# Two spare PSUM banks as working space for weight conversion and a product, in the last two blocks of a middle stage

## The chip, the cores and the metric

The kernel runs on one core of a Trainium2 chip. The metric is the device time of one execution in microseconds (us). Before the change the median of 3 runs is 1579.26 us (1579.03 to 1581.0).

## What is computed

Pooled attention feeds two groups of dense layers. In short:

```
k_p, v_p = mean of k, v over groups of 8 positions        # 576 -> 72 positions
attn     = softmax(q k_p^T / 8) v_p                       # 8 batches, 8 heads, 64 wide
x  = attn as 4608 tokens x 512
a  = x @ w1;  b = x @ w2                                  # 512 -> 1024
x2 = ((a * b) @ w3) @ w_out                               # 1024 -> 1024 -> 512
h  = x2 @ w_in2;  g = h * sigmoid(1.702 h)                # 512 -> 2048
out = g @ w_out2                                          # 2048 -> 512
```

The weights arrive in 64-bit floating point and are turned into 32-bit on the chip. Every 32-bit operand of a product is split in two parts, a rounded high part and the remainder, and each product is three matmuls (high by high, high by low, low by high).

## The kernel before

The program has three stages. The first converts and transposes the weights of the middle layers and runs the first attention groups. The middle stage (lines 547 to 588) goes over 9 blocks of 512 tokens; in each block it goes over 8 slices f of 128 features. For a slice TensorE makes `a` in PSUM bank `wk[0]` and `b` in bank `wk[1]`, 12 matmuls each (lines 566 to 568). ScalarE copies `a` to SBUF (line 573), VectorE multiplies it with `b` out of the bank (line 574), ScalarE writes the high part of the product to `u` and GpSimd the remainder (`split`, lines 95 to 97, called at line 576). Two slices later `x2_step` multiplies `u` with the folded weights into the four `acc` banks, 12 matmuls more. So a slice has 36 matmuls. Attention for later blocks runs between (`tick`) and uses banks `wk[2]` and `wk[3]`; it has ended when the last two blocks begin.

In the last two blocks the middle stage also converts the weights of the third stage: 16 tiles of `w_in2` in the first of the two and 16 of `w_out2` mostly in the second, two tiles a slice (`Conv.step`, lines 146 to 172). For one tile ScalarE scales the upper 32-bit words into a tile `w` in SBUF (line 154) and turns the lower words into integers (line 155); VectorE shifts `w` in place (line 156) and puts the sign bits in (line 159); GpSimd adds the low words (line 162). The tile then goes on a step later: `win_first` and `win_second` (lines 426 to 448) make sums and differences of quarter tiles (line 444), split them (lines 419 and 420) and store them to DRAM; `wout_done` (lines 450 to 456) splits and stores. The subtractions at 420 and 444 and half of those of `wout_done` are VectorE's, the others GpSimd's; both of their operands lie in SBUF.

The third stage (from line 599) takes the memory of the middle one. Its first matmuls need four tiles `g`, loaded at line 737, whose loads wait for the last stores of the middle stage (line 545).

Every engine works through its own instructions in a fixed order and waits on semaphores; DMA transfers are issued by SyncE, in order too. The order on each engine is made by a scheduler when the kernel is built, from the program and its own estimates of durations, so an edit in one line can reorder instructions around it on all engines.

Of the kernel before, what the change touches and what calls it, by code (L numbers as in the profile page):

```python
# [7 lines left out]
F32 = mybir.dt.float32  # L8
F32R = mybir.dt.float32r
U32 = mybir.dt.uint32  # L10
I32 = mybir.dt.int32
AF = mybir.ActivationFunctionType
ALU = mybir.AluOpType
# [9 lines left out]
def pooled_attention_moe_moe2(  # L23
# [18 lines left out]
    nc = tc.nc  # L42
# [11 lines left out]
    NB = NT // T  # L54
# [19 lines left out]
    wk = [ps_p.tile([P, T], F32, name=f"wk{i}", tag=f"bank{i + 4}") for i in range(4)]  # L74
# [7 lines left out]
    def take(shape=(P, 2, T), dtype=F32R):  # L82
        pool, i = free.pop(0)
        t = pool.tile(list(shape), dtype, name=f"s{i}", tag=f"s{i}")
        held[id(t)] = (t, pool, i)
        return t

    def give(*ts):
        for t in ts:
            free.append(held.pop(id(t))[1:])  # L90

    def f32(ap):
        return ap.bitcast(F32)

    def split(dst, src, lo_eng):
        nc.scalar.copy(dst[:, 0], src)  # L96
        lo_eng.tensor_tensor(out=dst[:, 1], in0=src, in1=f32(dst[:, 0]), op=ALU.subtract)  # L97
# [6 lines left out]
    def mm3(o, a, a_sl, b, b_sl, first, last):  # L104

        nc.tensor.matmul(o, a[:, 0, a_sl], b[:, 0, b_sl], start=first, stop=False)  # L106
        nc.tensor.matmul(o, a[:, 0, a_sl], b[:, 1, b_sl], start=False, stop=False)  # L107
        nc.tensor.matmul(o, a[:, 1, a_sl], b[:, 0, b_sl], start=False, stop=last)  # L108

    def col_tile(w, f):  # L110
        return w[:, 2 * f * P:2 * (f + 1) * P].rearrange("(c p) m -> p c m", p=P)

    def row_tile(w, f):
        return w[f * P:(f + 1) * P, :]

    def sl(i, n=P):
        return slice(i * n, (i + 1) * n)

    class Conv:
# [3 lines left out]
        def __init__(self):  # L123
            self.todo, self.staged, self.line = [], [], [None, None]
            self.depth, self.keep = 9, 3

        def add(self, src, turn, done):
            self.todo.append((src, turn, done))
# [17 lines left out]
        def step(self):  # L146

            new = None
            if self.staged:
                t, turn, done = self.staged.pop(0)  # L150
                lo_w, hi_w = t[:, :, 0], t[:, :, 1]
                w = cv_p[0].tile([P, T], F32, name="cv", tag="cv", bufs=4)
                wu = w.bitcast(U32)
                nc.scalar.activation(w, hi_w.bitcast(F32), AF.Copy, scale=2.0 ** -112)
                nc.scalar.activation(lo_w.bitcast(I32), lo_w, AF.Copy, scale=2.0 ** -29)
                nc.vector.tensor_scalar(  # L156
                    out=wu, in0=wu, scalar1=4, scalar2=1,
                    op0=ALU.logical_shift_left, op1=ALU.logical_shift_right)
                nc.vector.scalar_tensor_tensor(  # L159
                    out=wu, in0=hi_w, scalar=0x80000000, in1=wu,  # L160
                    op0=ALU.bitwise_and, op1=ALU.bitwise_or)
                nc.gpsimd.tensor_tensor(  # L162
                    out=w.bitcast(I32), in0=w.bitcast(I32), in1=lo_w.bitcast(I32), op=ALU.add)
                give(t)
                new = [w, turn, done]
            mid, old = self.line
            if mid and mid[1]:
                mid[0] = mid[1](mid[0])
            key = old[2](old[0]) if old else None
            self.line = [new, mid]  # L170
            self.load()
            return key
# [4 lines left out]
    conv = Conv()  # L177
    cv_p = [None]

    with pa_ctx:  # L180
# [7 lines left out]
            out=mask[:, 0], in_=mask[:, 0], compare_op=ALU.is_gt, fill=0.0,  # L188
            base=SK, pattern=[[0, D]], channel_multiplier=-1)
        nc.gpsimd.affine_select(  # L190
            out=mask[:, 1], in_=mask[:, 1], compare_op=ALU.is_ge, fill=0.0,
# [12 lines left out]
            out=ident, in_=ident, compare_op=ALU.is_equal, fill=0.0,  # L204
# [172 lines left out]
        def x_slot(j, c):  # L377
            if (j, c) not in xs:
                xs[j, c] = take()
            return xs[j, c]  # L380
# [3 lines left out]
        def tick():  # L384
            t = tick_n[0]
            tick_n[0] += 1
            n, s = divmod(t, 4)
            if s == 0:
                if 0 <= n - 1 < NG:
                    g4(n - 1)  # L390
                if n == 0:
                    g0(0)
            elif s == 1:
                if n < NG:
                    g1(n)
            elif s == 2:
                if 0 <= n - 1 < NG:
                    g6(n - 1)
                if n < NG:
                    g2(n)  # L400
                    g_va(n)
                if n + 1 < NG:
                    g0(n + 1)
            elif n < NG:
                g3(n)
                g_vb(n)
# [19 lines left out]
        def win_first(f):  # L426
            def done(w):
                hold[0] = w
                units(f, A11, A12, w, nc.vector)
            return done  # L430

        def win_second(f):
            def done(w):
                h = hold[0]
                a11, a12 = h[:, :HU], h[:, HU:]
                a21, a22 = w[:, :HU], w[:, HU:]
                units(f, A21, A22, w, nc.gpsimd)
                c = take((P, 2, T), F32)
                cs = c.rearrange("p a (b m) -> p (a b) m", b=2)
                for o, p0_, p1_, op, eng in (  # L440
                        (0, a21, a22, ALU.add, nc.vector), (2, a11, a21, ALU.subtract, nc.gpsimd),
                        (1, cs[:, 0], a11, ALU.subtract, nc.vector),
                        (3, a12, cs[:, 1], ALU.subtract, nc.gpsimd)):
                    eng.tensor_tensor(out=cs[:, o], in0=p0_, in1=p1_, op=op)
                units(f, S1, S2, c[:, 0], nc.vector)
                units(f, S3, S4, c[:, 1], nc.gpsimd)
                give(c)
            return done

        def wout_done(f):  # L450
            def done(w):
                t = take()
                split(t, w, nc.gpsimd if f % 2 else nc.vector)
                nc.sync.dma_start(wout_d[f], f32(t))
                give(t)
            return done
# [90 lines left out]
        for blk in range(NB):  # L547
            x = [x_slot(blk, c) for c in range(KM)]
            if blk == NB - 2:

                pa_ctx.close()
                pa = pa_ctx.enter_context(tc.tile_pool(name="pc", bufs=1, reuse_waits="tile"))
                cv_p[0] = pa
                free[:0] = [(pa, NSLOT + i) for i in range(NX)]
                for f in range(NP1):
                    conv.add(col_tile(w_in2, f), None, win_first(f))
                    conv.add(col_tile(w_in2, f + NP1), None, win_second(f))
                for f in range(NF2):
                    conv.add(row_tile(w_out2, f), None, wout_done(f))
                conv.depth, conv.keep = 5, 5  # L560
                conv.load()
            for f in range(NF1):
                if conv.busy():
                    conv.step()
                pa_, pb_ = wk[0], wk[1]
                for ps, w in ((pa_, w1_s[f]), (pb_, w2_s[f])):
                    for c in range(KM):
                        mm3(ps, w, sl(c), x[c], slice(0, T), c == 0, c == KM - 1)
                if blk == NB - 1:
                    give(w1_s.pop(f))  # L570
                    give(w2_s.pop(f))
                a = pa.tile([P, T], F32, name="a", tag="a", bufs=2)
                nc.scalar.copy(a, pa_)
                nc.vector.tensor_tensor(out=a, in0=pb_, in1=a, op=ALU.mult)  # L574
                u = u_s[blk, f] = take()
                split(u, a, nc.gpsimd)
                pend.append((blk, f))
                tick()
                if len(pend) > 2:
                    x2_step()  # L580
                tick()
                if conv.busy():
                    conv.step()
            give(*(xs.pop((blk, c)) for c in range(KM)))
# [14 lines left out]
    with tc.tile_pool(name="pb", bufs=1, reuse_waits="tile") as pb, \  # L599
# [146 lines left out]
        for f in range(NF2):  # L746
            bk = bank()
            w = ready.pop(("h", 0, f, 0))
# [23 lines left out]
        for pr in range(1, NPAIR + 1):  # L772
# [3 lines left out]
            for f in range(NP1):  # L776
# [10 lines left out]
                for name, u, b, first in ORDER:  # L787
                    o = B[b][1]
                    s, h = HS[u]
                    w = ready["h", pr, f, s]  # L790
# [90 lines left out]
```

## Time and profile before

| | |
|---|---|
| median of 3 runs | 1579.26 us |
| the profiled execution | 1577.45 us, of which its span is 1575.7 us |
| TensorE (PE) busy | 1500.1 us, 95% of the span |
| VectorE (DVE) busy | 1007.7 us, 64% |
| ScalarE (ACT), GpSimd (POOL) busy | 619.2 us, 617.0 us, 39% each |
| mean granted TensorE clock | 0.976 |

The span is the time from the first to the last instruction; what lies around it is 1.75 us here. TensorE is busy nearly throughout, so time is to be had only where it stands still or its granted clock is low. Times in the rows below are counted from the start of the span. The first of the last two blocks begins near 655 us and the middle stage ends near 816 us. The matmuls of a line overlap, so the distance of their starts, not their duration, is what one costs.

### The profile page before, as it was taken

The page shows a single profiled execution, that of the slowest core. Times are in us where ns is not written, and L with a number is a line of the kernel's source. Part 1 is how long each engine was busy: PE and PEld are TensorE (multiplying, and loading weights), DVE is VectorE, ACT ScalarE, POOL GpSimd, SP SyncE. Part 2 cuts the span into 40 slices and gives each one's busy share as a digit, 9 for nine tenths or more (in the row PEclk, how much of TensorE's full clock was granted, in tenths as well). Part 3 has the DMA queues.
Part 4 walks back from the last instruction along what each step waited for, and adds up shares of the span by engine and source line. Part 5 has one row for each costly group of instructions (what it writes and reads, how often), then busy time and mean ns, then how long its engine had stood idle before and what let it go on. Part 6 is the DMA issues. An engine that isn't in the chain of part 4 may idle for free.

```text
span 1575.7 us, 19586 instructions
## 1 busy us (share of the span) xinstructions
PE 1500.1 (95%) x6728; PEld 1233.7 (78%) x6728; DVE 1007.7 (64%) x1796; ACT 619.2 (39%) x1202; POOL 617.0 (39%) x674
## 2 busy tenths in 40 slices
PE   5976999999999999998979999999999999999998
PEld 3654888888888888876757888888888888888887
DVE  8999987878787877579754234462447244724441
ACT  6775443433333434355534222342225222522331
POOL 7789755444555554479752211100111011101110
PEclk9877999999999999999989999999999999999999
DMA  9972232323232310369769343432434234414310
GB/s 271 242 172 58 55 73 46 72 52 79 49 72 48 78 31 27 121 237 337 305 231 374 100 129 125 133 108 101 127 112 143 92 107 136 147 57 137 117 58 27
DMA packets 225444, 196.33 MB, mean 125 GB/s; under 512 B 158784, under 2 KB 175168, under 8 KB 225344
## 3 DMA queue, kind: packets, MB, share of 16 engines
q1 hardware_dynamic: 224768, 194.03, 41.3%
q8 instruction: 53, 0.87, 0.2%
q10 hardware_dynamic: 576, 1.05, 0.2%
q14 instruction: 47, 0.39, 0.1%
HBM read 150.99 MB, written 44.04 MB: 124 GB/s over the span
## 4 chain that ended last, share of the span: by engine, by line
PE 81%; DVE 8%; DMA 4%; issue 3%; POOL 1%; SPq 1%; ACT 1%; DVEq 0%; POOLq 0%; ACTq 0%
PE bk L644 22%; PE bk L108 8%; PE bk L107 8%; PE bk L106 8%; PE wk L108 7%; PE wk L106 7%; PE wk L107 7%; PE acc L108 3%; PE acc L107 3%; PE acc L106 3%; DVE cv L156 2%; PE wk L258 2%; DVE cv L159 2%; DMA s<-in_moe_w_dram 1%; DVE s L97 1%
## 5 line engine op out<-in xcount | busy, mean ns | idle before, releaser
L644 PE MATMUL bk<-xM,st 128*128 128x512 f32 x1344 | 319.1, 389 | 0.0
L644 PEld LDWEIGHTS bk<-xM,st 128*128 128x128 f32 x1344 | 252.3, 188 | 52.7 <-ACT o L661 0.4
L785 POOL TENSOR_TENSOR g<-g,sg 128x512 f32<-128x512 f32 x64 | 83.4, 1303 | 529.3 <-ACT sg L784 529.3
L106 PE MATMUL wk<-s,s 128*128 128x512 f32 x576 | 228.9, 399 | 15.0 <-DVE a L574 8.3
L107 PE MATMUL wk<-s,s 128*128 128x512 f32 x576 | 226.8, 394 | 2.0 <-DVE s L370 2.0
L108 PE MATMUL wk<-s,s 128*128 128x512 f32 x576 | 226.4, 394 | 1.4 <-DVE s L97 1.4
L107 PE MATMUL bk<-wo,mv 128*128 128x512 f32 x576 | 224.1, 389 | 0.0
L106 PE MATMUL bk<-wo,mv 128*128 128x512 f32 x576 | 223.9, 389 | 0.0
L108 PE MATMUL bk<-wo,mv 128*128 128x512 f32 x576 | 208.8, 389 | 0.0
L293 DVE STREAM_TRANSPOSE p<-s_t 32x160 f32<-32x160 f32 (+1 forms) x560 | 178.4, 319 | 10.8
L97 POOL TENSOR_TENSOR s<-a,s 128x512 fp32r<-128x512 f32 x72 | 96.6, 1341 | 185.6 <-ACT s L96 136.4
L106 PE MATMUL acc<-s,s 128*128 128x512 f32 x352 | 141.4, 407 | 7.1 <-ACT s L96 7.1
L108 PE MATMUL acc<-s,s 128*128 128x512 f32 x352 | 141.8, 403 | 5.1 <-DVE s L97 5.1
L107 PE MATMUL acc<-s,s 128*128 128x512 f32 x352 | 141.0, 400 | 0.9 <-POOL s L97 0.7
L106 PEld LDWEIGHTS wk<-s,s 128*128 128x128 f32 x576 | 108.8, 189 | 40.8 <-DVE a L574 10.6
L108 PEld LDWEIGHTS wk<-s,s 128*128 128x128 f32 x576 | 109.4, 190 | 24.8 <-DVE s L97 1.8
L107 PEld LDWEIGHTS wk<-s,s 128*128 128x128 f32 x576 | 109.5, 190 | 24.3 <-DVE s L370 2.4
L784 ACT ACTIVATE sg<-g 128x512 f32<-128x512 f32 x64 | 40.5, 633 | 217.0 <-DVE g L802 198.0
L107 PEld LDWEIGHTS bk<-wo,mv 128*128 128x128 f32 x576 | 108.1, 188 | 22.5
L106 PEld LDWEIGHTS bk<-wo,mv 128*128 128x128 f32 x576 | 108.1, 188 | 22.4
L108 PEld LDWEIGHTS bk<-wo,mv 128*128 128x128 f32 x576 | 108.1, 188 | 22.4
L162 POOL TENSOR_TENSOR cv<-cv,s 128x512 int32<-128x512 int32 x72 | 105.3, 1465 | 49.1 <-DVE cv L159 27.3
(139 smaller groups left out, 2401.3 us busy)
## 6 DMA issues: line engine op xcount, KB each, us to landing
st<-wind SPq DMA_DIRECT2D x112, 512.0 KB, 3.6
s<-in_moe_w_dram SPq DMA_DIRECT2D x32, 512.0 KB, 6.6
wind<-s SPq DMA_DIRECT2D x32, 512.0 KB, 4.5
s<-in_moe_w_out_dram SPq DMA_DIRECT2D x24, 512.0 KB, 7.8
kr<-in_k_dram SPq DMA_DIRECT2D x128, 72.0 KB, 2.5
qr<-in_q_dram SPq DMA_DIRECT2D x128, 72.0 KB, 2.5
out_dram<-o SPq DMA_DIRECT2D x36, 256.0 KB, 2.0
vr<-in_v_dram SPq DMA_DIRECT2D x32, 256.0 KB, 2.8
```

The costliest lines, as they stand in the source:

```text
L97: lo_eng.tensor_tensor(out=dst[:, 1], in0=src, in1=f32(dst[:, 0]), op=ALU.subtract)
L106: nc.tensor.matmul(o, a[:, 0, a_sl], b[:, 0, b_sl], start=first, stop=False)
L107: nc.tensor.matmul(o, a[:, 0, a_sl], b[:, 1, b_sl], start=False, stop=False)
L108: nc.tensor.matmul(o, a[:, 1, a_sl], b[:, 0, b_sl], start=False, stop=last)
L156: nc.vector.tensor_scalar(out=wu, in0=wu, scalar1=4, scalar2=1, op0=ALU.logical_shift_left, op1=ALU.logical_shift_right)
L159: nc.vector.scalar_tensor_tensor(out=wu, in0=hi_w, scalar=0x80000000, in1=wu, op0=ALU.bitwise_and, op1=ALU.bitwise_or)
L162: nc.gpsimd.tensor_tensor(out=w.bitcast(I32), in0=w.bitcast(I32), in1=lo_w.bitcast(I32), op=ALU.add)
L258: nc.tensor.matmul(sc[half][:, i * KW:(i + 1) * KW], qT[:, sl(tt)], mov, start=True, stop=True)
L293: nc.vector.transpose(out=dst[:, :nt, 32 * c:32 * c + 32], in_=s_t[32 * c:32 * c + 32, :nt, 32 * r:32 * r + 32])
L644: nc.tensor.matmul(o, w[:, x, m], b[:, y], start=first and n == 0, stop=last and n == 2, skip_group_check=True)
L784: nc.scalar.activation(sg, v, AF.Sigmoid, scale=1.702)
L785: eng.tensor_tensor(out=v, in0=v, in1=sg, op=ALU.mult)
```

## The change

Two things change, in the last two blocks alone. `Conv` gets a list `ps`, set to `wk[2:]` there, and uses its two banks in turn as the place `e` in which ScalarE puts the scaled words and VectorE shifts them; the instruction with the sign bits then reads `e` from PSUM and writes `w` in SBUF. And the product of `a` and `b` is written back over `b` in its bank; both parts of `u` are made from there, and the remainder is made by VectorE instead of GpSimd.

```
--- before.py
+++ after.py
@@ -123,6 +123,7 @@
         def __init__(self):
             self.todo, self.staged, self.line = [], [], [None, None]
             self.depth, self.keep = 9, 3
+            self.ps, self.n = [], 0
 
         def add(self, src, turn, done):
             self.todo.append((src, turn, done))
@@ -151,13 +152,17 @@
                 lo_w, hi_w = t[:, :, 0], t[:, :, 1]
                 w = cv_p[0].tile([P, T], F32, name="cv", tag="cv", bufs=4)
                 wu = w.bitcast(U32)
-                nc.scalar.activation(w, hi_w.bitcast(F32), AF.Copy, scale=2.0 ** -112)
+
+                e = self.ps[self.n % len(self.ps)] if self.ps else w
+                self.n += 1
+                eu = e.bitcast(U32)
+                nc.scalar.activation(e, hi_w.bitcast(F32), AF.Copy, scale=2.0 ** -112)
                 nc.scalar.activation(lo_w.bitcast(I32), lo_w, AF.Copy, scale=2.0 ** -29)
                 nc.vector.tensor_scalar(
-                    out=wu, in0=wu, scalar1=4, scalar2=1,
+                    out=eu, in0=eu, scalar1=4, scalar2=1,
                     op0=ALU.logical_shift_left, op1=ALU.logical_shift_right)
                 nc.vector.scalar_tensor_tensor(
-                    out=wu, in0=hi_w, scalar=0x80000000, in1=wu,
+                    out=wu, in0=hi_w, scalar=0x80000000, in1=eu,
                     op0=ALU.bitwise_and, op1=ALU.bitwise_or)
                 nc.gpsimd.tensor_tensor(
                     out=w.bitcast(I32), in0=w.bitcast(I32), in1=lo_w.bitcast(I32), op=ALU.add)
@@ -558,6 +563,7 @@
                 for f in range(NF2):
                     conv.add(row_tile(w_out2, f), None, wout_done(f))
                 conv.depth, conv.keep = 5, 5
+                conv.ps = wk[2:]
                 conv.load()
             for f in range(NF1):
                 if conv.busy():
@@ -571,9 +577,13 @@
                     give(w2_s.pop(f))
                 a = pa.tile([P, T], F32, name="a", tag="a", bufs=2)
                 nc.scalar.copy(a, pa_)
-                nc.vector.tensor_tensor(out=a, in0=pb_, in1=a, op=ALU.mult)
                 u = u_s[blk, f] = take()
-                split(u, a, nc.gpsimd)
+                if blk < NB - 2:
+                    nc.vector.tensor_tensor(out=a, in0=pb_, in1=a, op=ALU.mult)
+                    split(u, a, nc.gpsimd)
+                else:
+                    nc.vector.tensor_tensor(out=pb_, in0=pb_, in1=a, op=ALU.mult)
+                    split(u, pb_, nc.vector)
                 pend.append((blk, f))
                 tick()
                 if len(pend) > 2:
```

The scheduler reorders the engines. On VectorE, from the product of slice 4 of the first of the two blocks to that of slice 5 (line 574), there stood before (`wk_68` is the bank of `b`, `cv` a converted tile, the `s` tiles are parts in SBUF):

```order
L574 TENSOR_TENSOR a<-wk_68,a 128x512
L420 TENSOR_TENSOR s_6782<-cv,s_6782 128x2x256
L156 TENSOR_SCALAR cv<-cv 128x512
L444 TENSOR_TENSOR s_6840<-cv 128x256
L159 SCALAR_TENSOR_TENSOR cv<-s_6628,cv 128x512
L444 TENSOR_TENSOR s_6840<-s_6840,cv 128x256
L420 TENSOR_TENSOR s_6845<-s_6840,s_6845 128x2x256
L420 TENSOR_TENSOR s_6861<-cv,s_6861 128x2x256
L444 TENSOR_TENSOR s_6919<-cv 128x256
L574 TENSOR_TENSOR a<-wk_68,a 128x512
```

and there stands now, with the new line numbers (585 is the product; 161 and 164 are the shift and the sign bits, 425 and 449 the subtractions of 420 and 444, `wk_69` and `wk_70` the two spare banks):

```order
L585 TENSOR_TENSOR wk_68<-wk_68,a 128x512
L161 TENSOR_SCALAR wk_69<-wk_69 128x512
L161 TENSOR_SCALAR wk_70<-wk_70 128x512
L164 SCALAR_TENSOR_TENSOR cv<-s_6616,wk_69 128x512
L97 TENSOR_TENSOR s_6656<-wk_68,s_6656 128x512
L164 SCALAR_TENSOR_TENSOR cv<-s_6628,wk_70 128x512
L425 TENSOR_TENSOR s_6766<-s_6761,s_6766 128x2x256
L425 TENSOR_TENSOR s_6782<-cv,s_6782 128x2x256
L449 TENSOR_TENSOR s_6840<-cv 128x256
L161 TENSOR_SCALAR wk_70<-wk_70 128x512
L449 TENSOR_TENSOR s_6840<-s_6840,cv 128x256
L585 TENSOR_TENSOR wk_68<-wk_68,a 128x512
```

The remainder of `u` (the row of line 97) now stands three rows behind the product that it belongs to, and ahead of the next product.

At the end of the stage VectorE had, before:

```order
L159 SCALAR_TENSOR_TENSOR cv<-s_7233,cv 128x512
L156 TENSOR_SCALAR cv<-cv 128x512
L159 SCALAR_TENSOR_TENSOR cv<-s_7287,cv 128x512
L97 TENSOR_TENSOR s_7421<-cv,s_7421 128x512
L156 TENSOR_SCALAR cv<-cv 128x512
L159 SCALAR_TENSOR_TENSOR cv<-s_7299,cv 128x512
L97 TENSOR_TENSOR s_7513<-cv,s_7513 128x512
L574 TENSOR_TENSOR a<-wk_68,a 128x512
L544 COPY x2o<-acc_64 128x512
L544 COPY x2o<-acc_66 128x512
```

and now has:

```order
L161 TENSOR_SCALAR wk_70<-wk_70 128x512
L164 SCALAR_TENSOR_TENSOR cv<-s_7299,wk_70 128x512
L97 TENSOR_TENSOR s_7513<-cv,s_7513 128x512
L585 TENSOR_TENSOR wk_68<-wk_68,a 128x512
L97 TENSOR_TENSOR s_7389<-wk_68,s_7389 128x512
L585 TENSOR_TENSOR wk_68<-wk_68,a 128x512
L97 TENSOR_TENSOR s_7451<-wk_68,s_7451 128x512
L549 COPY x2o<-acc_64 128x512
L549 COPY x2o<-acc_66 128x512
```

The last conversions stand ahead of the products of the last two slices, which now follow one another, each with its remainder.

On TensorE the matmuls of `b` of a slice stood right behind those of `a` (`wk_67`), here for slice 7 of the last block:

```order
L106 MATMUL wk_67<-s_6276,s_1823 128x512
L107 MATMUL wk_67<-s_6276,s_1823 128x512
L108 MATMUL wk_67<-s_6276,s_1823 128x512
L106 MATMUL wk_68<-s_5764,s_1885 128x512
L107 MATMUL wk_68<-s_5764,s_1885 128x512
L108 MATMUL wk_68<-s_5764,s_1885 128x512
```

Now four matmuls with the high part of an earlier `u` stand between, here ahead of slice 6:

```order
L106 MATMUL wk_67<-s_6276,s_1823 128x512
L107 MATMUL wk_67<-s_6276,s_1823 128x512
L108 MATMUL wk_67<-s_6276,s_1823 128x512
L106 MATMUL acc_63<-s_7327,s_1127 128x512
L106 MATMUL acc_64<-s_7327,s_1127 128x512
L106 MATMUL acc_65<-s_7327,s_1127 128x512
L106 MATMUL acc_66<-s_7327,s_1127 128x512
L106 MATMUL wk_68<-s_5764,s_1820 128x512
L107 MATMUL wk_68<-s_5764,s_1820 128x512
```

In either order, for nearly all slices, 24 other matmuls lie between the last of one `b` and the first of the next: 12 of `a` and 12 of `x2_step`. Between slices 6 and 7 of the last block there are now 12.

## Rows read from the trace of the kernel before

**Rows 1.** Stretches: length, PE, PEld, DVE, ACT, POOL busy (count), PEclk, DMA share, GB/s

```profile
690.00:762.00 72.00, 61.72 (x258) 48.62 (x257) 66.23 (x63) 38.37 (x69) 65.21 (x47) 0.98 0.83 301
762.00:806.00 44.00, 43.11 (x189) 35.03 (x188) 37.44 (x35) 24.97 (x43) 34.42 (x23) 1.00 0.62 246
826.00:860.00 34.00, 31.94 (x127) 25.75 (x127) 12.16 (x17) 12.51 (x20) 7.97 (x6) 0.90 1.02 401
```

**Rows 2.** Waits of PE, 690 to 816 us: who waited for whom, total us, times, longest

```profile
PE wk L106 <- DVE a L574: 7.3, 5, 2.6
PE acc L106 <- ACT s L96: 4.0, 1, 4.0
PE wk L106 <- ACT a L573: 3.2, 2, 1.9
```

**Rows 3.** VectorE's groups, 690 to 754 us: shapes, count, busy us, mean ns, idle before

```profile
L159 DVE SCALAR_TENSOR_TENSOR cv<-s,cv 128x512 uint32<-128x512 uint32 x12 | 16.6, 1387 | 0.2
L156 DVE TENSOR_SCALAR cv<-cv 128x512 uint32<-128x512 uint32 x12 | 15.5, 1292 | 0.9 <-ACT cv L154 0.9
L420 DVE TENSOR_TENSOR s<-s,s 128x512 fp32r<-128x512 f32 x6 | 8.6, 1436 | 1.4 <-ACT s L419 1.4
L420 DVE TENSOR_TENSOR s<-cv,s 128x512 fp32r<-128x512 f32 x6 | 7.6, 1272 | 0.1
L444 DVE TENSOR_TENSOR s<-cv 128x256 f32<-128x256 f32 x6 | 5.8, 965 | 0.0
L444 DVE TENSOR_TENSOR s<-s,cv 128x256 f32<-128x256 f32 x6 | 5.7, 946 | 0.0
L574 DVE TENSOR_TENSOR a<-wk,a 128x512 f32<-128x512 f32 x6 | 4.1, 678 | 0.0
```

**Rows 4.** VectorE's lines, 655 to 812 us: ns min/median/max, first and last start

```profile
L574 DVE TENSOR_TENSOR a<-wk,a x16: 676/678/692, 663.1 to 806.9; 128x512 f32<-128x512 f32 x16
...
L156 DVE TENSOR_SCALAR cv<-cv x32: 414/1017/1539, 656.4 to 804.1; 128x512 uint32<-128x512 uint32 x32
...
L159 DVE SCALAR_TENSOR_TENSOR cv<-s,cv x32: 678/1113/1782, 656.9 to 805.7; 128x512 uint32<-128x512 uint32 x32
```

**Rows 5.** VectorE in order of time, 755 to 757 us: start us, us, instruction

```profile
755.23 0.68 DVE L159 SCALAR_TENSOR_TENSOR cv<-s,cv 128x512 uint32<-128x512 uint32 x1
755.83 0.68 DVE L420 TENSOR_TENSOR s<-s,s 128x512 fp32r<-128x512 f32 x1
756.43 0.69 DVE L544 COPY x2o<-acc 128x512 f32<-128x512 f32 x1
```

**Rows 6.** TensorE in order of time, 692 to 738 us

```profile
692.56 0.39 PE L108 MATMUL wk<-s,s 128*128 128x512 f32 x1
...
698.00 0.39 PE L108 MATMUL acc<-s,s 128*128 128x512 f32 x1
...
734.27 0.63 PE L107 MATMUL wk<-s,s 128*128 128x512 f32 x1
...
735.12 0.63 PE L106 MATMUL wk<-s,s 128*128 128x512 f32 x1
```

**Rows 7.** Four engines in order of time, 803 to 828 us

```profile
806.87 0.68 DVE L574 TENSOR_TENSOR a<-wk,a 128x512 f32<-128x512 f32 x1
...
808.65 0.61 ACT L96 CAST s<-a 128x512 fp32r<-128x512 f32 x1
...
809.31 2.07 PE L106 MATMUL acc<-s,s 128*128 128x512 f32 x4 [4.05 <-ACT s L96]
810.52 1.27 POOL L97 TENSOR_TENSOR s<-a,s 128x512 fp32r<-128x512 f32 x1
...
811.84 0.79 PE L107 MATMUL acc<-s,s 128*128 128x512 f32 x1 [0.46 <-POOL s L97]
...
814.99 0.63 PE L108 MATMUL acc<-s,s 128*128 128x512 f32 x1
...
821.23 2.56 PE L644 MATMUL bk<-g,st 128*128 128x512 f32 x5 [5.62 <-ACT g L101]
```

More of the change, by code (lines that the diff above doesn't have):

```diff
@@ L125, in __init__ @@
             self.depth, self.keep = 9, 3
+            self.ps, self.n = [], 0
         def add(self, src, turn, done):
@@ L153, in step @@
                 wu = w.bitcast(U32)
-                nc.scalar.activation(w, hi_w.bitcast(F32), AF.Copy, scale=2.0 ** -112)
+                e = self.ps[self.n % len(self.ps)] if self.ps else w
+                self.n += 1
+                eu = e.bitcast(U32)
+                nc.scalar.activation(e, hi_w.bitcast(F32), AF.Copy, scale=2.0 ** -112)
                 nc.scalar.activation(lo_w.bitcast(I32), lo_w, AF.Copy, scale=2.0 ** -29)
                 nc.vector.tensor_scalar(
-                    out=wu, in0=wu, scalar1=4, scalar2=1,
+                    out=eu, in0=eu, scalar1=4, scalar2=1,
                     op0=ALU.logical_shift_left, op1=ALU.logical_shift_right)
                 nc.vector.scalar_tensor_tensor(
-                    out=wu, in0=hi_w, scalar=0x80000000, in1=wu,
+                    out=wu, in0=hi_w, scalar=0x80000000, in1=eu,
                     op0=ALU.bitwise_and, op1=ALU.bitwise_or)
@@ L560, in pooled_attention_moe_moe2 @@
                 conv.depth, conv.keep = 5, 5
+                conv.ps = wk[2:]
                 conv.load()
@@ L573, in pooled_attention_moe_moe2 @@
                 nc.scalar.copy(a, pa_)
-                nc.vector.tensor_tensor(out=a, in0=pb_, in1=a, op=ALU.mult)
                 u = u_s[blk, f] = take()
-                split(u, a, nc.gpsimd)
+                if blk < NB - 2:
+                    nc.vector.tensor_tensor(out=a, in0=pb_, in1=a, op=ALU.mult)
+                    split(u, a, nc.gpsimd)
+                else:
+                    nc.vector.tensor_tensor(out=pb_, in0=pb_, in1=a, op=ALU.mult)
+                    split(u, pb_, nc.vector)
                 pend.append((blk, f))
```

## Prediction

> **What bounds the kernel now.** Start with the busy times by stretch: TensorE is full outside the end of the middle stage, but between 690 and 762 us it works 61.7 of 72 us, while VectorE is busy 66.2 and GpSimd 65.2 [rows 1]. The list of TensorE's waits says for whom: 7.3 us in five waits on the product (line 574), which alone frees the bank of `b`, and 3.2 us on the copy of `a` behind it in ScalarE's queue, 10.5 us together; then one wait of 4.0 us at the end [rows 2]. So VectorE's queue sets this stretch, and the question is why it is full. The list of its lines tells: the shift takes from 414 to 1539 ns and the sign bits from 678 to 1782 ns for the same shape, whereas the product, one operand in PSUM, takes 676 to 692 ns in all 16 cases, in the middle of the same crowd [rows 4]. What stretches are instructions whose inputs are all in SBUF, while GpSimd works there too. With no such neighbour they follow each other 0.60 us apart, start to start [rows 5].
>
> TensorE's own pace: 24 starts from 692.56 to 698.00 us, 0.227 us each [rows 6]. A slice of 36 is 8.2 us. After a wait the clock was low for a while: near 735 us two matmuls took 0.85 us [rows 6], 0.43 each; seven starts lie so, 1.4 us lost.
>
> The end is a chain: VectorE reaches the last product at 806.87, ScalarE rounds it at 808.65 behind conversions, GpSimd's remainder comes at 810.52 [rows 7]. TensorE waits 4.05 and 0.46 us and then runs its twelve last matmuls at the lower clock: from 809.31 to 814.99 are eleven distances [rows 7], 5.2 us without the wait, where 2.5 would do: 2.7 us lost. Then TensorE waits 5.62 us for the next stage's first tile [rows 7], whose load waits for the stage's last stores: this handover is not touched and moves with the end of the stage.
>
> **The change part by part.** *Shift and sign bits, 32 each.* In the dense stretch they took 1292 and 1387 ns [rows 3]. Out of PSUM the nearest rows are the copy from an accumulator, 0.69 us [rows 5], and the product, 678 ns [rows 3]; a shift that reads and writes PSUM is not in the trace. From below it could cost the quick form's 414 ns, from above what it cost, 1292 [rows 3, 4]. I take 0.68, or 0.60 from start to start, as for the other instructions with a PSUM input. Two tiles a slice: 5.36 us become 2.4.
>
> Here a rule speaks against the change. The quick shift takes 414 ns [rows 4], and a copy with a PSUM source 0.69 [rows 5]: on a VectorE alone the move would lose 0.27 us a tile. The Trainium skill (VectorE: DVE Perf Modes, "Why PSUM operands drop a tier") says that such an instruction loses its double rate with any PSUM operand. By the rule alone the 12 shifts of the dense stretch would add 3.3 us; by the measured mean of 1292 ns [rows 3] they give back 7.3. The trace decides for the second, as long as GpSimd is as busy as it is.
>
> *The remainder of `u`.* 16 instructions leave GpSimd, 1.27 us in quiet [rows 7], and come to VectorE at 0.60. GpSimd, 91% busy in the dense stretch [rows 1], gets free time by it, which shortens what VectorE's SBUF pairs wait for.
>
> *VectorE's sum for a dense slice.* Before: two shifts, two sign bits 5.36, four subtractions of lines 420 and 444 4.62, product 0.68: 10.7 us against TensorE's 8.2 [rows 3]. After: six instructions with PSUM at 0.60 are 3.6; the four subtractions keep both inputs in SBUF and stay exposed: from 0.60 and half of that [rows 5] to their means of 1.35 and 0.96 [rows 3], 1.9 to 4.6 us. I take 1.2 and 0.9, near the upper end, since GpSimd stays more than half busy: 4.2. Sum 7.8, between 5.5 and 8.2: below TensorE's 8.2 on average, hardly more.
>
> The subtraction of line 420 is 0.68 us in quiet [rows 5] and 1.27 to 1.44 in the crowd [rows 3]. The Trainium skill (SBUF — State Buffer, "Who interferes with whom") says that a VectorE instruction with two SBUF inputs meets GpSimd's reads on a shared port, and one with at most one SBUF input, outside the two-port modes, does not. By that rule the four stay at their upper prices as long as GpSimd works, the sum is 8.2 us and the first rival below does not come; the product's 676 to 692 ns [rows 4] are the other half of it.
>
> *The bank of `b` is held longer.* Until now the product freed it; now the rounding on ScalarE and the remainder must follow. In quiet that is 0.68 + 0.61 + 0.69 [rows 4, 5, 7], with handovers some 2.2 us; 24 matmuls, 5.4 us, cover it. But the remainder stands in VectorE's queue behind others. The dense slices walked in the new order, at the prices above: between the products of slices 2 and 3 stand 18 instructions, 11 at 0.60, four at 0.9, three at 1.2, with the product 14.4 us, where TensorE needs 50 matmuls, 11.3: product 3 is 3.1 late. Its remainder comes four later, 4.8 with product and remainder: 7.9 us after the last matmul of `b`, against 26 matmuls, 5.9: TensorE waits 2.0. Product 4 comes 6.0 after it, `b` of slice 4 takes 2.7, so 3.3 late; remainder 4 follows in 3.0, at 6.3 against 5.4: 0.9. Slice 5 gives 0.6 and slice 6 nothing. Together 3.5. With only two banks ScalarE can't run ahead: where a shift follows the sign bits of the same bank, VectorE sits through one ScalarE instruction, 0.6 us; 1.5 for that. So 5 of the 10.5 us remain.
>
> *The end.* Behind the last `b` stand eight matmuls of the slice before, 1.8 us, then four that need the rounded part, then those that need the remainder, and no GpSimd work is in that chain any more. In quiet, product and rounding take 1.3 to 1.5 and the remainder 2.2: hidden. Between slices 6 and 7 only 12 matmuls, 2.7 us, cover the bank. But the last conversions stand ahead of both products, so I leave 1 us of the 4.5. With so short a wait the clock should stay up: the 2.7 us go.
>
> *Elsewhere.* At the block border the accumulator copies and the first tiles now share VectorE with remainders: 1 us of new wait. SyncE's transfers are the same, in another order; 301 GB/s in the dense stretch against 401 where it ran full [rows 1] leaves room for a stretch shorter by a tenth.
>
> Sum: waits 10.5 to 5, -5.5; end 4.5 to 1, -3.5; slow matmuls at the end -2.7; border +1; the low spell of 1.4 us I keep, since a wait is left that can bring it. That is -10.7 on the profiled execution's 1577.45 (span 1575.7 and 1.75 around it): 1566.8. The median of the runs is 1.8 above the profiled one, so 1568.5.
>
> **The rivals.** *All waits go.* If the four subtractions fall to 0.60 and 0.3, the sum for a slice is 5.5 us, the remainder never comes late, and all of 10.5 + 4.5 + 2.7 + 1.4 = 19.1 us go: 1560. For it: 1.27 us of GpSimd's work a slice leave. Against: of GpSimd's 47 instructions from 690 to 762 us [rows 1] only eight go.
>
> *The wait changes its name.* The bank's longer hold, the two-bank turn and ScalarE's queue (it came to the last rounding 1.1 us after the product was ready [rows 7]) leave the dense stretch at its 10.5; only the end gains, 3.5 + 2.7 less 1: 1574. For it: the cover of 5.4 us was not enough for one pass through the queue, and two are needed now.
>
> *Slower: the PSUM forms wait like the others.* If VectorE's shift and sign bits stay as slow as they are in this crowd, each slice gets the remainder on top: 11.3 us, or 12.5 for a slice with three shifts as slice 4 has, instead of 10.7; over seven slices 4 to 12 us, and the end stays late: 1583 to 1591, say 1586. It decides from 1.19 us a piece on, where the four no longer give back the 0.60. Against: the product's 16 equal rows [rows 4], but none of them writes PSUM.
>
> **How the numbers follow.** The forecast gets 0.60, with 1563 to 1574 as its own range; all waits gone 0.12; the changed name 0.16; slower 0.12. The range 1560 to 1578 takes in the second and third and leaves the slower case out. What a measurement can tell from no change is 0.2%, 3.2 us: faster means below 1576.1. Faster holds the forecast, the first rival and half of the second, 0.80; the same, the other half and a mild case of the slower one, 0.11; slower 0.09.
>
> **What would show it.** Right: shift and sign bits at 0.65 to 0.72 us in every case, at least 20 us less work on GpSimd (16 times 1.27), VectorE's product no longer the releaser but the remainder of `u`, waits of TensorE of 3 to 7 us between 690 and 760, no wait above 1.5 us at the stage's end and the stage over some 10 us earlier, with the third stage as long as before. Wrong: shifts above 1 us; TensorE waits of 2 us in each slice for line 97; or the time won at the end of the stage lost to later loads in the next.

## The result and the profile after

The changed kernel takes 1561.77 us (median of 5 runs, 1560.15 to 1564.58); the kernel before, run beside it, 1579.26 (5 runs, 1576.79 to 1581.39). The ratio is 0.9889, 95% interval 0.9873 to 0.9905: 17.5 us less, between 15 and 20. The forecast was 1568.5, so the direction holds and the size was put too low by 6.7 us; the time lies below the 1563 to 1574 that the forecast gave as its own range, and inside the 1560 to 1578 of the whole.

The profiled execution of the changed kernel took 1564.58 us (span 1562.9), the slowest of its five, and the two profiled executions differ by only 12.9. The first thing to settle is why. Two rows of the first stage, 100 to 200 us, code that the change does not touch; first the kernel before, then the one after (columns as in [rows 1]):

```profile
100.00:200.00 100.00, 78.22 (x336) 60.91 (x334) 95.52 (x185) 49.15 (x109) 81.10 (x99) 0.82 0.30 58
```

```profile
100.00:200.00 100.00, 80.09 (x327) 61.63 (x327) 95.74 (x180) 47.45 (x106) 78.72 (x97) 0.76 0.29 54
```

The granted clock is 0.82 against 0.76 and nine matmuls fewer are done. At the start of the changed stretch the profiled execution is 2.7 us late: a slice's matmuls that begin at 648.20 us in the one trace begin at 650.92 in the other. The variants below have the same first stage, and their profiles show either value: 0.82 in five of them, 0.76 or 0.77 in three and in a second profile of the changed kernel, 0.80 in one. The early loads of `x2` alone, an edit in the third stage, show 0.76 in the kernel before and 0.82 in the changed one. So it does not come with the change; what brings it about is not shown. Without it the pair differs by 15.6, inside the interval of the runs.

Now the stretches that the prediction spoke of. TensorE's rows after, answering to [rows 1]:

```profile
690.00:762.00 72.00, 69.70 (x304) 56.24 (x303) 57.71 (x75) 43.11 (x77) 53.11 (x42) 1.00 0.97 371
762.00:806.00 44.00, 38.81 (x170) 31.51 (x169) 27.76 (x38) 22.51 (x39) 25.34 (x20) 1.00 0.58 221
826.00:860.00 34.00, 30.32 (x121) 24.28 (x120) 18.63 (x27) 13.23 (x23) 6.10 (x4) 0.90 0.78 300
```

In the dense stretch TensorE works 69.7 of 72 us instead of 61.7, with 304 matmuls instead of 258. GpSimd falls from 65.2 to 53.1 and VectorE, which got more instructions (75 for 63), from 66.2 to 57.7. TensorE's waits, 640 to 860 us, answering to [rows 2]:

```profile
PE bk L654 <- ACT g L101: 4.6, 2, 3.0
PE bk L654 <- DMA st<-wind: 3.7, 1, 3.7
PE acc L106 <- ACT s L96: 2.5, 2, 2.2
PE wk L106 <- DVE s L97: 1.2, 2, 0.8
PE wk L106 <- ACT a L579: 0.8, 1, 0.8
```

The product has left the list. The last three rows are all that the middle stage keeps: 2.3 us in the dense stretch (before 10.5) and one wait of 2.2 at the end. What became of the instructions, answering to [rows 4] and [rows 3] (line 161 is the old 156, 164 the old 159, 425 the old 420, 449 the old 444):

```profile
L161 DVE TENSOR_SCALAR wk<-wk x32: 680/687/700, 659.7 to 789.7; 128x512 uint32<-128x512 uint32 x32
```

```profile
L164 DVE SCALAR_TENSOR_TENSOR cv<-s,wk x32: 668/678/689, 660.5 to 790.5; 128x512 uint32<-128x512 uint32 x32
```

```profile
L449 DVE TENSOR_TENSOR s<-cv 128x256 f32<-128x256 f32 x6 | 7.4, 1230 | 0.0
L425 DVE TENSOR_TENSOR s<-s,s 128x512 fp32r<-128x512 f32 x7 | 6.8, 978 | 0.0
L425 DVE TENSOR_TENSOR s<-cv,s 128x512 fp32r<-128x512 f32 x5 | 6.6, 1311 | 1.1 <-ACT s L424 1.1
L449 DVE TENSOR_TENSOR s<-s,cv 128x256 f32<-128x256 f32 x6 | 6.0, 996 | 0.1
```

Shift and sign bits now take 668 to 700 ns in all 64 cases, where they took 414 to 1782. The four subtractions, which keep two SBUF inputs, are still exposed: means of 1.0 to 1.3 us, before 0.9 to 1.4 [rows 3]. VectorE hardly waits for its input with the two banks, 0.7 us for ScalarE's scaling between 690 and 754 us:

```profile
L161 DVE TENSOR_SCALAR wk<-wk 128x512 uint32<-128x512 uint32 x14 | 9.4, 687 | 0.8 <-ACT wk L159 0.7
```

The end of the stage in order of time, answering to [rows 7]:

```profile
790.46 0.69 DVE L164 SCALAR_TENSOR_TENSOR cv<-s,wk 128x512 uint32<-128x512 uint32 x1
...
791.61 1.10 DVE L97 TENSOR_TENSOR s<-cv,s 128x512 fp32r<-128x512 f32 x1 [0.46 <-ACT s L96]
792.64 0.68 DVE L585 TENSOR_TENSOR wk<-wk,a 128x512 f32<-128x512 f32 x1
793.36 0.58 ACT L96 CAST s<-wk 128x512 fp32r<-128x512 f32 x1 [1.78 <-DVE wk L585]
...
794.00 1.21 PE L106 MATMUL acc<-s,s 128*128 128x512 f32 x4 [2.21 <-ACT s L96]
...
805.47 0.96 PE L654 MATMUL bk<-g,st 128*128 128x512 f32 x3 [2.98 <-ACT g L101]
...
809.62 13.54 PE L654 MATMUL bk<-g,st 128*128 128x512 f32 x51 [1.57 <-ACT g L101]
...
841.54 8.65 PE L654 MATMUL bk<-g,st 128*128 128x512 f32 x25 [3.67 <-DMA st<-wind]
```

The last conversion still stands ahead of the product in VectorE's queue (the subtraction at 791.61), so TensorE waits 2.21 us. Then the clock stays up: the four matmuls behind the wait take 1.21 us, before 2.07. The first matmul of the third stage waits 2.98 us instead of 5.62, but two later waits there grew, 1.39 to 1.57 and 2.06 to 3.67, and one of 0.39 is new. From its first matmul to the end the third stage takes 757.4 us, before 754.5.

### The profile page after: what moved, and what is told of

The parts are those of the page before. It is cut to its first block, busy times and chain, and to the rows that moved or that the text cites. A ratio compares the mean times of both kernels' runs of the same rounds, so it can differ in the third digit from the quotient of the medians.

```text
span 1562.9 us, 19560 instructions
## 1 busy us (share of the span) xinstructions
PE 1499.4 (96%) x6728; PEld 1234.3 (79%) x6728; DVE 984.4 (63%) x1812; ACT 618.7 (40%) x1202; POOL 586.1 (38%) x658
## 4 chain that ended last, share of the span: by engine, by line
PE 80%; DVE 11%; DMA 3%; issue 2%; ACT 1%; SPq 1%; POOL 1%; DVEq 0%; ACTq 0%; POOLq 0%
PE bk L654 22%; PE bk L107 8%; PE bk L106 8%; PE bk L108 8%; PE wk L106 7%; PE wk L108 7%; PE wk L107 7%; PE acc L106 3%; PE acc L107 3%; PE acc L108 3%; PE wk L263 2%; DVE cv L164 2%; DVE p L298 2%; DVE s L97 2%; DMA wo<-woutd 1%
## 5 line engine op out<-in xcount | busy, mean ns | idle before, releaser
L108 PE MATMUL acc<-s,s 128*128 128x512 f32 x352 | 141.4, 402 | 5.1 <-DVE s L97 4.9
L107 PE MATMUL acc<-s,s 128*128 128x512 f32 x352 | 140.5, 399 | 0.4 <-POOL s L97 0.3
L106 PE MATMUL acc<-s,s 128*128 128x512 f32 x352 | 134.3, 404 | 5.4 <-ACT s L96 5.4
L97 POOL TENSOR_TENSOR s<-a,s 128x512 fp32r<-128x512 f32 x56 | 72.4, 1293 | 176.6 <-ACT s L96 135.8
L167 POOL TENSOR_TENSOR cv<-cv,s 128x512 int32<-128x512 int32 x72 | 101.2, 1412 | 64.4 <-DVE cv L164 26.6
```

The lines of the kernel that those rows point to most:

```text
L167: nc.gpsimd.tensor_tensor(out=w.bitcast(I32), in0=w.bitcast(I32), in1=lo_w.bitcast(I32), op=ALU.add)
```

## The experiments

All were timed beside the kernel before; the ratios are to it. Each variant was put in order anew by the scheduler, so orders differ along with what was edited.

**Conversion alone.** The product and the remainder of `u` go back to the old form.

```diff
+                nc.vector.tensor_tensor(out=a, in0=pb_, in1=a, op=ALU.mult)
                 u = u_s[blk, f] = take()
-                if blk < NB - 2:
-                    nc.vector.tensor_tensor(out=a, in0=pb_, in1=a, op=ALU.mult)
-                    split(u, a, nc.gpsimd)
-                else:
-                    nc.vector.tensor_tensor(out=pb_, in0=pb_, in1=a, op=ALU.mult)
-                    split(u, pb_, nc.vector)
+                split(u, a, nc.gpsimd)
```

> Only the conversion goes through the two spare banks; product in SBUF and remainder on GpSimd as before. Theory (VectorE's shift and sign bits were stretched because their inputs all lay in SBUF while GpSimd worked there): both at 0.67 to 0.70 us in every case, waits of TensorE from 690 to 760 us under 4 us instead of 10.5, the end of the stage still a wait of 2 to 4.5 us on GpSimd's remainder and some slow matmuls: 8 to 13 us less than before. Rival (the gain comes from taking 16 remainders off GpSimd): under 4 us less than before.

Measured: 1563.1, ratio 0.9907 (0.9892 to 0.9923). TensorE's waits in the middle stage:

```profile
PE wk L106 <- DVE a L580: 2.9, 3, 1.3
PE acc L107 <- POOL s L97: 0.8, 1, 0.8
```

Nearly all of the gain is here, more than the 8 to 13 us expected. With shift and sign bits at 0.68 to 0.69 us TensorE never waits more than 1.3 us for the product, though GpSimd keeps the remainder; the wait of 2 to 4.5 us expected at the end of the stage is 0.8. These 3.7 us are even less than the changed kernel's 4.5. That the second part adds anything is not shown: the ratios differ by 0.18%, 2.8 us, and the medians by 1.3, but the intervals overlap. The traces do not decide it: SyncE is past the last converted tile's store at 798.47 us here and at 796.32 in the changed kernel, and the third stage's first matmul starts at 808.83 against 805.47, yet the span is 1561.4 us here and 1562.9 and 1561.2 in two profiles of the changed kernel, all three with the low clock in the first stage.

**Product and remainder alone.** Conversion stays in SBUF.

```diff
-                conv.ps = wk[2:]
```

> Only the product is written over b in its bank and the remainder made by VectorE; the conversion stays in SBUF. Theory: shift and sign bits stay stretched, at means of 1.0 us or more, and VectorE gets 0.6 us more per slice while the bank of b is held longer: dense waits of 8 to 20 us, the end better by 4 to 7; in all between 3 us less and 8 us more than before. Rival (GpSimd's relief is the gain): 10 us or more less than before.

Measured: 1582.22, ratio 1.0023 (1.0013 to 1.0033): slower. VectorE's two conversion lines, 690 to 754 us, and TensorE's waits:

```profile
L164 DVE SCALAR_TENSOR_TENSOR cv<-s,cv 128x512 uint32<-128x512 uint32 x13 | 18.5, 1425 | 0.3
L161 DVE TENSOR_SCALAR cv<-cv 128x512 uint32<-128x512 uint32 x12 | 10.1, 840 | 0.0
```

```profile
PE acc L106 <- ACT s L96: 10.7, 5, 4.8
PE wk L106 <- ACT a L578: 4.9, 1, 4.9
PE wk L106 <- DVE s L97: 4.1, 3, 2.1
```

The remainder leaves GpSimd for a VectorE that is still full, and `b`'s bank is held through that queue: 19.7 us of waits. It is the slower rival of the prediction in kind, reached by leaving out the part that makes room. One expectation missed: sign bits stay stretched, but the shift's mean falls from 1292 to 840 ns without any bank, beside a GpSimd that is busy 56.3 us from 690 to 762 us instead of 65.2. The order on TensorE does not make the gain either: this variant has its groups of matmuls nearly as the changed kernel has them, four with the high part between `a` and `b`, and is some 20 us slower. The two parts do not add: -0.93% and +0.23% would be -0.70%, and together they give -1.11%.

**Is it GpSimd, and is it the PSUM operand?** In the trace of the kernel before, 9 of the 32 instructions with the sign bits ran while GpSimd had none in progress: 679 to 693 ns each. The 13 that lay wholly within GpSimd's work took 1106 to 1782. One of the latter, with the first of the two GpSimd instructions that it met:

```profile
717.60 1.50 POOL L162 TENSOR_TENSOR cv<-cv,s 128x512 int32<-128x512 int32 x1
717.96 1.69 DVE L159 SCALAR_TENSOR_TENSOR cv<-s,cv 128x512 uint32<-128x512 uint32 x1
```

In the changed kernel 22 of the shifts and 16 of the sign bits lay as wholly within it, at 668 to 700 ns. Two variants give one instruction each two SBUF inputs again. In the first the product goes back to SBUF, and the remainder stays on VectorE; in the second the shift writes to SBUF, so that the sign bits read both inputs there.

```diff
-                    nc.vector.tensor_tensor(out=pb_, in0=pb_, in1=a, op=ALU.mult)
-                    split(u, pb_, nc.vector)
+                    nc.vector.tensor_tensor(out=a, in0=pb_, in1=a, op=ALU.mult)
+                    split(u, a, nc.vector)
```

> Conversion through the spare banks; the product stays in SBUF, so it alone frees the bank of b, and VectorE makes the remainder from there with two SBUF inputs. Theory of the longer hold (the 2.3 us of dense waits left in the changed kernel come from it): no wait of TensorE on the remainder, dense waits under 1.5 us, and 16 to 20 us less than before although the remainder is stretched to 0.9 to 1.3 us. Rival (VectorE's throughput sets what is left): dense waits of 3 us or more, 12 to 16 us less than before.

```diff
-                    out=eu, in0=eu, scalar1=4, scalar2=1,
+                    out=wu, in0=eu, scalar1=4, scalar2=1,
...
-                    out=wu, in0=hi_w, scalar=0x80000000, in1=eu,
+                    out=wu, in0=hi_w, scalar=0x80000000, in1=wu,
```

> As the changed kernel, but the shift writes its result to SBUF, so the sign bits have both inputs there again. Theory (two SBUF inputs are enough to be stretched): sign bits at a mean of 1.0 us or more, the shift at 0.68; a dense slice of VectorE 8.5 to 9.2 us, dense waits of 4 to 8 us; 9 to 15 us less than before. Rival (only the shift, in its quick double form, met GpSimd): sign bits at 0.68 us, 16 us or more less than before.

Measured: 1564.04, 0.9906 (0.9892 to 0.9921), and 1569.39, 0.9941 (0.9926 to 0.9955). VectorE, 690 to 754 us; the remainder in the first, then sign bits and shift in the second:

```profile
L97 DVE TENSOR_TENSOR s<-a,s 128x512 fp32r<-128x512 f32 x7 | 7.6, 1092 | 2.1 <-ACT s L96 2.1
```

```profile
L164 DVE SCALAR_TENSOR_TENSOR cv<-s,cv 128x512 uint32<-128x512 uint32 x13 | 14.3, 1117 | 0.0
L161 DVE TENSOR_SCALAR cv<-wk 128x512 uint32<-128x512 uint32 x13 | 8.6, 682 | 0.8 <-ACT wk L159 0.7
```

The sign bits go from 677 back to 1117 ns by that one operand, while the shift beside them, PSUM to SBUF, keeps 682: what exposes an instruction beside GpSimd is that all it reads is in SBUF. That operand takes back 0.52% of the 1.11%, some 8 us; the 9.2 us less that remain are as expected. The Trainium skill (SBUF — State Buffer, "Who interferes with whom") says that a VectorE instruction with two SBUF inputs meets GpSimd's reads of SBUF and that one with at most one, outside the two-port modes, does not: the trace agrees, 1117 against 677 ns. The first variant missed its expectation of 16 to 20 us less: the bank of `b` came free earlier, but TensorE waits 4.5 us on the product, which is now late behind remainders of 1.09 us, and the gain of 14.6 us falls in the rival's range. VectorE's throughput, not the bank, sets what is left there; in time the variant is not told apart from the changed kernel.

**Banks.** The changed kernel again, then one bank for the conversions instead of two, then besides it two banks for `b` by turns.

```diff
-                conv.ps = wk[2:]
+                conv.ps = wk[3:]
```

```diff
-                pa_, pb_ = wk[0], wk[1]
+                pa_, pb_ = wk[0], wk[1 + f % 2 if blk >= NB - 2 else 1]
```

> The changed kernel once more, to have it beside the next three on one chip: ratio 0.987 to 0.991 to the kernel before, about 1562. Two bound readings of its size: if 17 us is right, 1561 to 1563; if the profiled pair's 13 us is right, 1564 to 1566.

> The conversions go through one spare PSUM bank instead of two in turn. Theory A (the two-bank turn costs nothing on the path: VectorE sat 0.7 us in the whole dense stretch on ScalarE's scaling): with one bank the scaling must wait for the sign bits of the tile before, so each of the two shifts of a slice waits some 0.7 to 1.2 us for ScalarE, 1.4 to 2.4 us a slice; VectorE has about 2 us a slice to spare against TensorE's 8.2, so TensorE's waits in the dense stretch grow from 2.3 to 3 to 6 us, and the run is 1 to 4 us above the changed kernel. Theory B (my forecast's 1.5 us for two banks was right in kind: a shortage of banks goes to the path in full): 6 to 10 us above the changed kernel.

> One spare bank for the conversions as in e5, and the other one lets b change between two banks in the last two blocks, so that the next b need not wait for the remainder of the slice before. Theory A (the waits that remain are the longer hold of b's bank): no wait of TensorE on line 97 or 96 is left between 690 and 800, 2 to 4 us less than e5, near the changed kernel or 1 us below it. Theory B (VectorE's throughput is what is short): the waits move to x3's tiles or to the converted weights and the time is that of e5 within 1 us.

Measured on one chip: 1560.64, 1562.55 and 1560.87; ratios 0.989 (0.9874 to 0.9907), 0.9901 (0.9884 to 0.9919), 0.9892 (0.9875 to 0.9909). The times differ by little more than their spread (1560.62 to 1562.92, 1561.86 to 1565.36, 1560.76 to 1563.47), but the traces do not. TensorE's waits, 650 to 830 us, with one bank, then with two for `b`:

```profile
PE bk L654 <- ACT g L101: 12.5, 1, 12.5
PE wk L106 <- DVE s L97: 2.0, 1, 2.0
PE acc L106 <- ACT s L96: 1.4, 2, 1.1
```

```profile
PE bk L654 <- ACT g L101: 14.9, 1, 14.9
PE wk L106 <- ACT a L579: 1.7, 2, 1.3
```

One bank costs the dense stretch less than 1 us, so the two-bank turn costs next to nothing there. With two banks for `b` no wait for the remainder is left and the stage's last matmul ends at 796.04 us, 6.4 before the changed kernel's 802.49 (2.6 of it from the earlier start described above), and all of that is lost to a wait of 14.9 us for the third stage's first tile.

**The start of the third stage.** Why it does not follow is in SyncE's queue. Rows of it from the changed kernel, then from the one with two banks for `b`:

```profile
762.10 34.13 SPq L459 DMA_DIRECT2D woutd<-s  x13
796.32 1.99 SPq L634 DMA_DIRECT2D st<-wind  x3
798.83 8.85 SPq L747 DMA_DIRECT2D g<-x2d  x4
```

```profile
792.53 7.12 SPq L459 DMA_DIRECT2D woutd<-s  x4
799.75 2.46 SPq L634 DMA_DIRECT2D st<-wind  x3
802.25 2.43 SPq L747 DMA_DIRECT2D g<-x2d  x4
```

The loads stand behind the stores of the last converted tiles, and these wait for VectorE and GpSimd (36 us of SyncE's waits on line 459). With one bank the conversions finish 3 to 6 us later. Two variants put the loads of `x2` (line 747) behind one weight tile instead of three; the second has the banks of the last one too. A third does the same to the kernel before.

```diff
-        for _ in range(3):
-            pull()
+        pull()
...
-        for _ in range(3, NST):
+        for _ in range(1, NST):
             pull()
```

> The changed kernel, with one thing else at the start of the third stage: the four loads of x2 are issued behind the first weight tile's load, not behind three of them. Theory A (the third stage's start is bound by bytes: 400 GB/s from 800 to 850 us): the wait for the first tile falls from 3.0 to 0.5 to 1.5 us, and the later waits on weight tiles (3.7 us) grow by as much; the time stays within 1 us of the changed kernel, and the first store of the third stage is where it was, near 907.8. Theory B (order, not bytes, costs the handover): both waits fall, 2 to 4 us less.

> Two banks for b and one for the conversions (as e6), and the early loads of x2 (as e7). Theory A (e6's stage ended at 796.1 but its third stage waited 14.9 us for a load that stood behind three others; order is what costs): the wait falls to 4 to 8 us, the two gains add, 1551 to 1555, ratio 0.983 to 0.985. Theory B (the bytes before the third stage set its start, at some 805 us whenever the stage ends): no better than e7, 1556 to 1559.

> The kernel before, with the early loads of x2 alone: it tells whether the wait between the stages was there all along or came with the change. Theory A (it was there: the first tile and the two later waits were 5.6, 1.4 and 2.1 us in the kernel before, and with the late loads the third stage never starts better): 3 to 5 us less than before, ratio 0.9965 to 0.998. Theory B (it came with the earlier end of the stage, which the loads cannot follow): within 1.5 us of before.

Measured: 1557.5 (1555.6 to 1558.62), ratio 0.9865 (0.9849 to 0.9882); 1559.79, 0.9869 (0.9855 to 0.9884); 1573.88, 0.9967 (0.9955 to 0.9979). The third stage's first matmuls in the first of them:

```profile
803.29 0.50 PE L654 MATMUL bk<-g,st 128*128 128x512 f32 x1 [2.01 <-ACT g L101]
804.64 1.15 PE L654 MATMUL bk<-g,st 128*128 128x512 f32 x2 [0.84 <-POOL g L102]
807.01 11.87 PE L654 MATMUL bk<-g,st 128*128 128x512 f32 x40 [1.22 <-ACT g L101]
```

The three waits come to 4.1 us where the changed kernel has four with 8.6, and the wait on a weight tile did not grow but went: in the changed kernel order cost this, not bytes. The loss was there before the change, since the kernel before gains 0.33% by the same edit. The loads of `x2` first make the best kernel here: its runs lie below all runs of the changed kernel on the same chip (1560.62 and above), 3.1 us by the medians. With the two banks for `b` nothing is added, where 1551 to 1555 was expected: the stage ends at 796.45 us, but its last conversion leaves SyncE at 800.14, against 793.66, and TensorE waits 12.1 us. SyncE's rows with the early loads alone, then with the banks too:

```profile
793.66 0.38 SPq L634 DMA_DIRECT2D st<-wind  x1
796.78 6.91 SPq L746 DMA_DIRECT2D g<-x2d  x4
```

```profile
800.14 0.52 SPq L634 DMA_DIRECT2D st<-wind  x1
800.75 2.93 SPq L746 DMA_DIRECT2D g<-x2d  x4
```

The first of the four loads is issued 4.0 us later with the banks, and it lands 7.1 us after its issue instead of 3.1, though one weight tile stands before it in both. The DMA engines are full then, a share of 1.01 from 800 to 804 us and 0.95 from 804 to 808, so half of its 8.0 us of delay goes to the slower transfer and not to order. Over all profiles the first matmul of the third stage comes 8.4 to 12.1 us after SyncE issues its first weight load (6.7 in the kernel before with the early loads), but 2.0 to 14.9 us after TensorE's last matmul of the middle stage. So this start follows SyncE's queue, that is the end of the conversions, more closely than TensorE's end. No run moved the end of the conversions and nothing else, so that this sets it is argued and not shown.

## Why the prediction came out, and where its sum was off

The mechanism held: VectorE's queue filled by instructions whose inputs are all in SBUF, PSUM operands that shield them. Its terms, against the pair of profiles with the 2.7 us of the first stage taken out:

- *Shift and sign bits at 0.68 us*: measured 668 to 700 ns. Right. By the rule on the lost double rate alone (the Trainium skill, VectorE: DVE Perf Modes, "Why PSUM operands drop a tier") 12 shifts would have cost 3.3 us more. The rule itself the trace bears out, 680 to 700 ns out of PSUM against 414; against the sum it decides, since the quick 414 ns was rarely had here (median 1017 [rows 4]).
- *The releaser changes from the product to the remainder*: right, line 97 is in the list and the product is not. GpSimd's work falls from 617.0 to 586.1 us, 31 less where at least 20 were asked: the 16 remainders had stretched themselves, at a mean of 1.5 us, and some 7 us are shorter stretching of the others.
- *Dense waits 10.5 to 5*: 10.5 to 2.3, the largest miss, 2.7 us. The forecast held 1.5 us for the turn with two banks; VectorE sat 0.7 us on ScalarE's scaling between 690 and 754 us, and a bank less changed under 1 us. The other 1.2 are the walk: product 3 started 2.0 us after the start of the last matmul of its `b` instead of 3.1, and its bank was free after 6.7 instead of 7.9 us. The subtractions, priced at 1.2 and 0.9, were 1.0 to 1.3, so their price is not what was wrong.
- *The low-clock spell of 1.4 us kept*: it went. No wait above 0.8 us is left in the dense stretch, and the granted clock there is 1.00, before 0.98.
- *Block border, +1 us*: nothing was seen there.
- *End wait 4.5 to 1*: 2.2, 1.2 us too hopeful. I had named the conversions ahead of the last product and priced them too low.
- *Slow matmuls at the end, -2.7*: gone, as forecast.
- *The handover is not touched and moves with the end*: its waits come to 9.1 us before and 8.6 after, so the number was right; the reason holds only by half. The first tile's load does not wait for the stores of line 545, as the text ahead of the prediction has it: in the trace of the kernel before SyncE issued it at 813.58 us, when a converted tile's store (line 454) had landed, and the first of those stores was issued, by ScalarE, at 813.77. Loads behind it waited for them, 7.0 us in two waits. So the first tile follows the last stores of converted tiles (SyncE past them at 810.99 before and at 796.32 after, 14.7 us earlier), and TensorE's end moved 13.1. That they moved together was luck; the variant with two banks for `b` parts them.
- *The third stage as long as before*: 2.9 us longer in this pair from its first matmul on, 2.2 of it in its later waits; from TensorE's last matmul of the middle stage on it is 760.4 us, before 760.1.

These corrections, 2.7, 1.4 and 1.0 more and 1.2 less, bring 10.7 to 14.6; 1.0 of the 15.6 I could not assign. The remaining 1.9 up to the 17.5 of the medians lies within their interval. Three terms, the two-bank turn, the low spell and the border, thus cost little or nothing that the runs show, and the end wait was priced too low. Two of the signs that were named missed in the same way: waits of 2.3 us in the dense stretch where 3 to 7 were named, and one of 2.2 at the end where at most 1.5 was. The rival that all waits go (1560) was nearer in size, for another reason than it gave: the subtractions did not fall to 0.60.

## What to carry to other kernels

Where VectorE and GpSimd share a stretch, look at the spread of each VectorE line, not its mean: a line that varies by two or three times beside one that never varies tells which operands are exposed, and moving one input to PSUM can be worth more than the instruction's slower quiet form costs. Moving work onto the engine that is full cost 0.23% here; after that engine had been relieved it cost nothing, and whether it then gained is not shown. Test the parts apart. Before shortening a stage further, ask which queue starts the next one: here ending TensorE's stage some 4 us earlier won nothing, and four loads moved ahead in SyncE's queue won 3 us.

## What the runs showed of the hardware that was not expected

The shield is complete here: 64 instructions, 38 of them wholly within GpSimd's work, lie within 668 to 700 ns, with one SBUF input or none, and the shift costs the same whether its output goes to PSUM (687 ns) or to SBUF (682). Remainder and sign bits with two SBUF inputs cost 1.09 to 1.43 us on average in the same stretch. GpSimd's own instructions are shortened too when VectorE's are shielded: with the conversion alone, where GpSimd keeps all its work, its sum of the low words takes 1432 ns instead of 1571 from 690 to 754 us, and its whole busy time is 609.2 us instead of 617.0. And profiles of kernels with the same first stage differ by 2.7 us from a stretch of that stage alone, with a granted clock of 0.82 or 0.76 there, enough to hide or feign a small gain in a pair of profiles.
